# First loads of a fused attention and FFN kernel: x0 in column halves, value weights right behind it, and a new order of the first TensorE steps

## The chip, the cores and the metric

The kernel runs on one core of one Trainium2 chip. The metric is the device time of one execution in microseconds (us); lower is better. Five engines work from queues of their own: TensorE (PE in the profile), VectorE (DVE), ScalarE (ACT), GpSimd (POOL) and SyncE (SP). SP and ACT also issue the DMA transfers.

## What is computed

Two branches over the same tokens x (2048 x 640, bf16), mixed by a gate for each token:

```python
def _A_ref(x, wqkv, w_phi, wo):                      # linear attention, 32 heads of 20
    qkv = transpose(reshape(x @ wqkv, (B, S, 3, H, Dh)), (2, 0, 3, 1, 4))
    q, k, v = qkv
    pq = einsum("bhsd,hdf->bhsf", q, w_phi);  pk = einsum("bhsd,hdf->bhsf", k, w_phi)
    phi_q = concat([softmax(pq), softmax(-pq)]);  phi_k = concat([softmax(pk), softmax(-pk)])
    kv = einsum("bhsf,bhsd->bhfd", phi_k, v);  z = einsum("bhsf->bhf", phi_k)
    o = einsum("bhqf,bhfd->bhqd", phi_q, kv) / (einsum("bhqf,bhf->bhq", phi_q, z) + 1e-6)
    return o_as_rows @ wo

g = sigmoid((x * gate_w).sum(-1))
a = _A_ref(x, wqkv, w_phi, wo)
b = (silu(x @ w_gate) * (x @ w_up)) @ w_down         # F = 1728
out = g * a + (1 - g) * b
```

## The kernel before

The 2048 tokens are 16 tiles of 128, and the 640 features are five slices of 128. The value weights `wvg` hold five rows of tiles `w0` to `w4` (128 x 640 each, 160 KB), one for each slice of features, and one more column for the gate weight. A value tile V of a token tile is then ten matmuls: for each slice c, one of 320 columns (half 0) and one of 321 columns (half 1, which ends with the gate column), both with slice c of the transposed tokens `xT` as weights.

Two strings at the top of the file fix the order. `LOADS` (L33) is the order in which the loads are issued; each item goes to the queue that `XQ`, `WQ` (L391, L392) or its own function names. `ORDER` (L38) is the order in which the compute steps are recorded; every engine runs its instructions in that order. A tracker puts semaphore waits in front of an instruction for what it reads and writes. It tracks PSUM by whole banks and SBUF by byte ranges, so that the gate column of `wvg` is apart from the rest.

The steps at the start of `ORDER`:

- `H` (`warm`, L511): two matmuls of 128 x 128 on a constant, whose result nobody reads. There are 13 of these steps, so 26 matmuls.
- `X` (`xpose`, L495): transposes a token tile on TensorE. The first four tiles are loaded by rows (`load_x`, L399) and transposed this way; the other twelve are loaded by DMA transposes (`load_xt`). For tiles 0 to 2 the transposes are two parts, slice 0 and slices 1 to 4, in two PSUM banks, and each part has a copy into `xT`. `X0.0` is the first part of tile 0 and `X0.1` the second; the copies run on DVE, that of `X0.1` on ACT.
- `G` (`gcol`, L505): one matmul that turns the gate row `gwr` (loaded as 5 x 128, item `g`) into a column, and a DVE copy of it into `wvg`'s last column.
- `U` (`vpart`, L539): `Ut.c` is slice c of the value tile of token tile t, two matmuls. The tiles 0 to 2 are made in these parts, interleaved as the weights arrive.
- `h` (`load_phi`, L417): issues two small loads from ACT, behind a wait for the row tile `w3`.

PSUM is handed out as four pairs of banks by a ring (`next_pair`, L489), each step taking the pair used longest ago; an accumulating `U` tile holds its pair until its last part.

The loads of the first microseconds, by queue, in order of issue: SP has x0, g, w1, w2, w3, then the first 384 columns of the FFN weights (`f0`: wg, wu), then the DMA transposes (`k0`, `k1`, `t4` and so on). ACT has w0, x1, x2, x3, w4. A DMA issue occupies its queue for some 0.4 us.

After the start, TensorE runs through the key weights (`M`: blocks of w_phi times the transposed wqkv), the FFN's first half (`F`), keys, queries and the output steps. These are not touched.

Of the kernel before, what the change touches and what calls it, by code (L numbers as in the profile page):

```python
# [6 lines left out]
P = 128  # L7
S_TOK = 2048
D = 640
# [21 lines left out]


LOADS = """  # L33
x0 w0 x1 g w1 x2 w2 x3 w3 w4 f0 k0 k1 t4 k2 k3 k4 k5 t5 t6 t7 t8 t9 t10 t11 t12 t13 t14 t15 q0 q1 q2 q3 q4 q5
 f1 f2
"""

ORDER = """  # L38
H0 H1 H2 H3 H4 H5 H6 H7 H8 H9 H10 H11 H12 X0.0 G X0.1 X1 h U0.0 U1.0 U0.1 X2 U1.1 U2.0 U0.2 U1.2
U2.1 X3 U2.2 U0.3 U1.3 U2.3 U0.4 U1.4 U2.4 V3 Y i4 F0.1 M0 M1 F0.2 M2 V4 M3 M4 F0.0 M5 K0 i3 K1 S0 I  # L40
P0 K3 S1 P1 F1.0 K2 V6 E0 V8 K4 S2 S3 E1 S4 K5 S5 P2 P3 V7 E2 V5 R0 K6 P4 P5 R2 E3 K7 S6 E4 V15 K8
E5 V10 S7 P6 K9 E6 R1 P7 S8 K10 S9 E7 K11 S10 V9 V11 P8 E8 K12 P9 R3 E9 P10 K13 S11 E10 K14 S12 P11
# [11 lines left out]
class _Tracker:  # L54
# [90 lines left out]
    def run(self, eng, fn, reads=(), writes=(), dma=False):  # L145
        rkeys = list(dict.fromkeys(k for a in reads for k in self.keys_of(a)))
        wkeys = list(dict.fromkeys(k for a in writes for k in self.keys_of(a)))
        need = {}

        def req(ev, raw):  # L150
            if ev is None:
                return
            s, v = ev
            if s == eng and not dma and (eng == "pe" or not raw):
                return
            if v > need.get(s, 0):
                need[s] = v

        for k in rkeys:
            for kk in self._conflicts(k):  # L160
                req(self.lastw[kk], True)
                if k[0] == "psum":
                    for s, v in self.readers[kk].items():
                        req((s, v), False)
        for k in wkeys:
            for kk in self._conflicts(k):
                req(self.lastw[kk], True)
                for s, v in self.readers[kk].items():
                    req((s, v), False)
        self._wait(eng, need)  # L170
        ins = fn()
        if dma:
            sn = "d%d" % self.ndma
            self.ndma += 1
            self._add_sem(sn)
            inc = 16
        else:
            sn, inc = eng, 1
        ins.then_inc(self.sem[sn], inc)
        self.cnt[sn] += inc  # L180
        v = self.cnt[sn]
        snap = dict(self.known[eng])
        if not dma:
            snap[sn] = max(snap.get(sn, 0), v)
        self.evknow.setdefault(sn, {})[v] = snap
        ev = (sn, v)
        for k in wkeys:
            self.lastw[k] = ev
            self.readers[k] = {}
        for k in rkeys:  # L190
            r = self.readers[k]
            if r.get(sn, 0) < v:
                r[sn] = v
        return ev


def _build(nc, A_x, A_wqkv, A_w_phi, A_wo, B_x, B_w_gate, B_w_up, B_w_down, gate_w, out):
    tr = _Tracker(nc)
    pe, act, dve, pool, sp = nc.tensor, nc.scalar, nc.vector, nc.gpsimd, nc.sync
# [83 lines left out]
    def at(name, shape, dtype, rel):  # L283
        n = mybir.dt.size(dtype)
        for s in shape[1:]:
            n *= s
        assert rel + n <= SLAB, (name, rel + n, SLAB)
        t = nc.alloc_sbuf_tensor_at(name, list(shape), dtype, offset=sbase + rel)
        tr.reg(t, "sbuf", sbase + rel)
        return t  # L290
# [4 lines left out]
    xs = at("xs", [P, NPE, D], BF16, 10752)  # L295
# [10 lines left out]
    def bank(b, c0, c1, r0=0, r1=P):  # L306
        return ps[r0:r1, b * 512 + c0:b * 512 + c1]
# [9 lines left out]
    def mm(pairs):  # L317
        reads, writes = [], []
        for p in pairs:
            reads += [p[1], p[2]]  # L320
            writes.append(p[0])

        def fn():
            last = None
            for o, l, r, st, sp_, sk in pairs:
                last = pe.matmul(o, lhsT=l, rhs=r, start=st, stop=sp_, skip_group_check=sk)  # L326
            return last
        return run("pe", fn, list({id(a): a for a in reads}.values()), writes)
# [45 lines left out]
    def dma(e, dst, src, transpose=False):  # L374
        eo = tr.eng[e]

        def fn():
            if transpose:
                return eo.dma_start_transpose(dst, src)
            return eo.dma_start(dst, src)  # L380
        rd = [src] if src.tensor.name in tr.base else []
        wr = [dst] if dst.tensor.name in tr.base else []
        return run(e, fn, rd, wr, dma=True)
# [4 lines left out]
            channel_multiplier=cm), [ap], [ap])  # L388


    XQ = ["sp", "act", "act", "act"]  # L391
    WQ = ["act", "sp", "sp", "sp", "act"]  # L392
    x2 = A_x[0]
    out2 = out[0]

    def load_rows(e, dst, c, c0):
        return dma(e, dst, A_wqkv[c * P:(c + 1) * P, c0:c0 + D])

    def load_x(t):  # L399
        dma(XQ[t], xs[:, t, :], x2[t * P:(t + 1) * P, :])  # L400

    def load_xt(t):
        dma("sp", xT[:, t, :, :], x2[t * P:(t + 1) * P, :], transpose=True)
# [7 lines left out]
    def load_wv(c):  # L411
        wv_evs.append(load_rows(WQ[c], wvg[:, c, 0:D], c, 2 * D))

# [70 lines left out]
    def used(r):  # L484
        ring["lru"].remove(r)
        ring["lru"].append(r)
        return r

    def next_pair():  # L489
        return used([r for r in ring["lru"] if r < ring["n"] and r not in held][0])  # L490
# [31 lines left out]
    def v_pairs(t, pr):  # L522
        return [(bank(2 * pr + hb, 0, 320 + hb), xT[:, t, c, :], wvg[:, c, 320 * hb:640 + hb - 320 * (1 - hb)],
                 c == 0, c == 4, False) for c in range(5) for hb in range(2)]

    def v_out(t, pr):
        i = halves(pr).rearrange("p b (h d) -> p b h d", d=DH)
        o = vbuf(t)[:, 0:H * (DH + 1)].rearrange("p (b h d) -> p b h d", b=2, d=DH + 1)[:, :, :, 0:DH]
        copy("act", o, i)
        copy("act", svec[:, t:t + 1], bank(2 * pr + 1, 320, 321))  # L530
# [6 lines left out]
    vpr = {}  # L537

    def vpart(t, c):  # L539

        if c == 0:
            vpr[t] = next_pair()
            held.add(vpr[t])
        mm(v_pairs(t, vpr[t])[2 * c:2 * c + 2])
        if c == 4:
            held.remove(used(vpr[t]))
            v_out(t, vpr[t])
# [398 lines left out]
    def kv_end():  # L946
# [4 lines left out]

    ops = {
        "H": lambda i: warm(), "i": fills, "X": xpose, "G": gcol, "U": vpart, "V": vtile,
        "M": lambda m: premult(1, m), "R": lambda m: premult(0, m),
        "K": ktile, "S": knorm, "P": kmul, "p": lambda t: kmul(t, "dve"), "E": kvtile, "x": load_x, "t": load_xt, "w": load_wv, "g": load_gate, "h": load_phi, "k": lambda m: load_wt(1, m), "q": lambda m: load_wt(0, m),
        "f": lambda i: load_ffn(FCUT[i], FCUT[i + 1]), "L": load_late_weights, "T": tail_weights, "J": gates,
        "Y": w_blocks, "I": kv_begin, "N": kv_end, "Z": z_row,
# [9 lines left out]
def bass_gated_mix__linear_kernel_hedgehog__swiglu_ffn__prompt_kernel(  # L967
    nc: bass.Bass,
    A_x: bass.AP,
    A_wqkv: bass.AP,  # L970
    A_w_phi: bass.AP,
    A_wo: bass.AP,
    B_x: bass.AP,
    B_w_gate: bass.AP,
    B_w_up: bass.AP,
    B_w_down: bass.AP,
    gate_w: bass.AP,
    out: bass.AP,
):
    _build(nc, A_x, A_wqkv, A_w_phi, A_wo, B_x, B_w_gate, B_w_up, B_w_down, gate_w, out)  # L980
# [28 lines left out]
```

## Time and profile before

| | us |
|---|---|
| median of 3 runs | 285.96 (285.23 to 286.51) |
| the profiled execution, its own time | 286.04 |
| its span, first to last instruction | 284.8 |
| first TensorE instruction starts (warm matmuls) | 0.84 |
| first transpose of x0 starts | 3.85 |
| last matmul of the program ends, about | 282.9 |
| DVE busy | 193.2 |
| POOL busy | 155.3 |
| ACT busy | 139.6 |

The span is the time from the first to the last instruction on the chip. The measured time of the same execution is 1.2 us longer. An engine's busy time is the union of its instructions; the profile models the end of a pipelined matmul, so the pace of TensorE is better read from start to start. The granted clock in the profile's rows is 1.00 in every slice.

The loads at the start, from issue to landing: x0 is issued on SP at 0.81 and takes 3.0 us, w0 on ACT at 0.80 and takes 3.2, w4 as the last of the row loads on ACT at 2.70 and takes 5.3. The first FFN weights are issued at 3.00 and 3.48 and take 6.2 and 7.2 us.

### The profile page before, as it was taken

The numbers are of one execution on the slowest core, as the hardware profiler recorded it, in microseconds if no ns is written. First come the engines' busy times: TensorE is split into PE (matmuls) and PEld (weight loads), VectorE is DVE, ScalarE is ACT, GpSimd is POOL, SyncE is SP. The second block draws the span as 40 slices with busy tenths as digits, with TensorE's granted clock in tenths as the row PEclk, the third lists the DMA queues.
The fourth block names the chain that finished last, engine by engine and source line by source line (L and its number), as shares of the span: only waits on it lengthen the run. The fifth ranks groups of instructions, "written<-read, shape, count | busy, mean of one in ns | idle before, by whom it ended". The sixth has DMA issues, their size and how long they took to land.

```text
span 284.8 us, 4696 instructions
## 1 busy us (share of the span) xinstructions
PE 281.9 (99%) x1809; PEld 156.8 (55%) x1809; DVE 193.2 (68%) x280; ACT 139.6 (49%) x241; POOL 155.3 (55%) x119
## 2 busy tenths in 40 slices
PE   8999999999999999999999999999999999999997
PEld 6666777766645445445545444554544444444766
DVE  1346667784789998979999899997878355053100
ACT  2477687786755666657746764130101675001022
POOL 6276988888167859597858744463062553100100
PEclk9999999999999999999999999999999999999999
DMA  7986679200065362022330200623547520133411
GB/s 231 232 104 129 109 136 370 86 3 0 3 218 185 78 107 51 9 52 53 60 52 3 52 4 10 138 51 71 115 139 138 76 61 7 41 78 73 122 46 46
DMA packets 62085, 25.19 MB, mean 88 GB/s; under 512 B 51023, under 2 KB 61543, under 8 KB 62063
## 3 DMA queue, kind: packets, MB, share of 16 engines
q1 hardware_dynamic: 60534, 24.03, 37.7%
q10 hardware_dynamic: 1529, 0.87, 1.1%
q8 instruction: 14, 0.23, 0.4%
q14 instruction: 8, 0.07, 0.1%
HBM read 10.16 MB, written 2.63 MB: 45 GB/s over the span
## 4 chain that ended last, share of the span: by engine, by line
PE 98%; DMA 1%; DVE 0%; issue 0%
PE ps L326 97%; DMA xs<-in_A_x_dram 1%; PE ps L338 1%; DVE osb L934 0%
## 5 line engine op out<-in xcount | busy, mean ns | idle before, releaser
L354 POOL TENSOR_TENSOR hT<-hT,us 128x512 bf16<-128x512 bf16 (+1 forms) x37 | 42.9, 1167 | 43.5 <-DVE hT L358 33.2
L326 PE MATMUL ps<-xT,wg 128*128 128x512 bf16 x260 | 64.6, 379 | 0.0
L326 PE MATMUL ps<-xT,wu 128*128 128x512 bf16 x260 | 64.6, 379 | 0.0
L354 POOL TENSOR_TENSOR ph<-eq,qc 128x1320 bf16<-128x1320 bf16 x16 | 40.3, 2521 | 31.0 <-DVE qc L673 19.8
L326 PE MATMUL ps<-wqk,xT 128*128 128x320 bf16 x320 | 47.9, 299 | 0.0
L344 ACT ACTIVATE us<-ps 128x512 bf16<-128x512 f32 (+1 forms) x56 | 33.4, 597 | 22.0 <-PE ps L326 19.8
L326 PEld LDWEIGHTS ps<-xT,wu 128*128 128x128 bf16 x260 | 25.4, 98 | 30.7
L326 PEld LDWEIGHTS ps<-xT,wg 128*128 128x128 bf16 x260 | 25.0, 98 | 28.4 <-ACT oT L344 0.6
L354 POOL TENSOR_TENSOR ekr<-ekr,krec 128x1280 bf16<-128x1280 bf16 x16 | 37.3, 2358 | 5.8 <-DVE krec L368 5.8
L344 ACT ACTIVATE eq<-ps 128x640 bf16<-128x640 f32 x32 | 22.3, 703 | 32.3 <-PE ps L326 31.2
L358 DVE SCALAR_TENSOR_TENSOR hT<-hT,ps 128x512 bf16<-128x512 bf16 (+1 forms) x37 | 25.0, 681 | 19.1 <-ACT hT L344 17.5
L326 PEld LDWEIGHTS ps<-wqk,xT 128*128 128x128 bf16 x320 | 30.4, 98 | 13.3
L354 POOL TENSOR_TENSOR hx<-hx,us 128x512 bf16<-128x512 bf16 (+1 forms) x19 | 24.1, 1272 | 22.1 <-DVE hx L358 16.3
L344 ACT ACTIVATE hT<-ps 128x512 bf16<-128x512 f32 (+1 forms) x37 | 22.0, 596 | 25.0 <-PE ps L326 24.8
L326 PE MATMUL ps<-hT,wd 128*128 128x512 bf16 (+1 forms) x140 | 31.1, 379 | 0.0
L365 DVE TENSOR_REDUCE ksum<-ekr 128x64 f32<-128x1280 bf16 x16 | 23.4, 1464 | 11.0 <-ACT ekr L344 11.0
L344 ACT ACTIVATE ekr<-ps 128x640 bf16<-128x640 f32 x32 | 22.3, 703 | 6.9 <-PE ps L326 6.4
L326 PE MATMUL ps<-wvg,xT 128*128 128x320 bf16 (+1 forms) x160 | 24.7, 305 | 0.0
L365 DVE TENSOR_REDUCE qw<-ez 128x64 f32<-128x1280 bf16 x16 | 23.6, 1476 | 0.0
L365 DVE TENSOR_REDUCE qz<-eq 128x64 f32<-128x1280 bf16 x16 | 23.6, 1478 | 0.0
L354 DVE TENSOR_TENSOR ez<-eq,zb 128x1280 bf16<-128x1280 bf16 x16 | 22.9, 1449 | 0.6 <-DMA zb<-zrow 0.6
L326 PEld LDWEIGHTS ps<-hT,wd 128*128 128x128 bf16 (+1 forms) x140 | 13.0, 97 | 16.1 <-issue 1.3
(103 smaller groups left out, 291.2 us busy)
## 6 DMA issues: line engine op xcount, KB each, us to landing
wd<-in_B_w_down_dram SPq DMA_DIRECT2D x1, 2080.0 KB, 10.3
out_dram<-osb SPq DMA_DIRECT2D x2, 640.0 KB, 3.5
wg<-in_B_w_gate_dram SPq DMA_DIRECT2D x1, 1040.0 KB, 8.6
wu<-in_B_w_up_dram SPq DMA_DIRECT2D x1, 1040.0 KB, 9.8
wog<-in_A_wo_dram SPq DMA_DIRECT2D x2, 375.0 KB, 4.1
wg<-in_B_w_gate_dram SPq DMA_DIRECT2D x1, 640.0 KB, 5.0
wu<-in_B_w_up_dram SPq DMA_DIRECT2D x1, 640.0 KB, 6.3
omgb<-omgd SPq DMA_DIRECT2D x2, 256.0 KB, 4.0
```

The costliest lines, as they stand in the source:

```text
L326: last = pe.matmul(o, lhsT=l, rhs=r, start=st, stop=sp_, skip_group_check=sk)
L338: last = pe.transpose(o, i, ident[0:k, 0:k])
L344: return run("act", lambda: act.activation(o, i, func, scale=scale), rd, [o])
L354: return run(e, lambda: eo.tensor_tensor(o, a, b, op), [a, b], [o])
L358: return run("dve", lambda: dve.scalar_tensor_tensor(out=o, in0=a, scalar=s, in1=b, op0=op0, op1=op1), rd, [o])
L365: return run("dve", lambda: dve.tensor_reduce(o, i, AX.X, ALU.add), [i], [o])
```

## The change

```diff
 LOADS = """
-x0 w0 x1 g w1 x2 w2 x3 w3 w4 f0 k0 k1 t4 ...
+x0 w0 w1 x1 g x2 w2 x3 w3 w4 f0 k0 k1 t4 ...

 ORDER = """
-H0 H1 H2 H3 H4 H5 H6 H7 H8 H9 H10 H11 H12 X0.0 G X0.1 X1 h U0.0 U1.0 U0.1 X2 U1.1 U2.0 U0.2 U1.2
+H0 H1 H2 H3 H4 H5 H6 H7 H8 H9 H10 H11 X0.0 X0.1 G U0.0 U0.1 X1 h U1.0 X2 U1.1 U2.0 U0.2 U1.2

-    XQ = ["sp", "act", "act", "act"]
-    WQ = ["act", "sp", "sp", "sp", "act"]
+    XQ = ["sp", "act", "act", "sp"]
+    WQ = ["act", "sp", "sp", "sp", "sp"]

     def load_x(t):
-        dma(XQ[t], xs[:, t, :], x2[t * P:(t + 1) * P, :])
+        if t == 0:
+            for e, c0, c1 in (("sp", 0, 384), ("act", 384, D)):
+                dma(e, xs[:, t, c0:c1], x2[t * P:(t + 1) * P, c0:c1])
+        else:
+            dma(XQ[t], xs[:, t, :], x2[t * P:(t + 1) * P, :])

     def vpart(t, c):
...
-        mm(v_pairs(t, vpr[t])[2 * c:2 * c + 2])
+        vp = v_pairs(t, vpr[t])[2 * c:2 * c + 2]
+        for m in ([vp[0:1], vp[1:2]] if t == c == 0 else [vp]):
+            mm(m)
```

Tile x0 is loaded in two parts: columns 0 to 383 (98 KB) at the head of SP's queue, columns 384 to 639 (66 KB) at the head of ACT's. By queue the order is now: SP has x0's first part, w1, g, w2, x3, w3, w4, wg, wu and then the DMA transposes; ACT has x0's second part, w0, x1, x2. So x3 and w4 have moved from ACT to SP.

On TensorE there are 24 warm matmuls instead of 26. The two parts of tile 0's transposes follow each other, G comes behind them, then both matmuls of U0.0 and of U0.1, then X1, then U1.0. From X2 on the order is the old one. U0.0's two matmuls are two groups with waits of their own: the first reads half 0 of `w0`, the second half 1 and the gate column. With one H step less, the ring hands other pairs of banks to the steps behind; the number of pairs and their order of reuse are the same.

More of the change, by code (lines that the diff above doesn't have):

```diff
@@ L33 @@
 LOADS = """
-x0 w0 x1 g w1 x2 w2 x3 w3 w4 f0 k0 k1 t4 k2 k3 k4 k5 t5 t6 t7 t8 t9 t10 t11 t12 t13 t14 t15 q0 q1 q2 q3 q4 q5
+x0 w0 w1 x1 g x2 w2 x3 w3 w4 f0 k0 k1 t4 k2 k3 k4 k5 t5 t6 t7 t8 t9 t10 t11 t12 t13 t14 t15 q0 q1 q2 q3 q4 q5
  f1 f2
```

## The prediction, made before the changed kernel was run

> **What bounds the kernel now.** I read the page first, for the engine shares, then the chain of waits, then the timeline of the first 13 us, because the diff touches nothing later. The page, and under it the chain in order of time (start, length, what):
>
> ```profile
> PE 281.9 (99%) x1809; PEld 156.8 (55%) x1809; DVE 193.2 (68%) x280; ACT 139.6 (49%) x241; POOL 155.3 (55%) x119
> ```
>
> ```profile
> 0.81 3.00 DMA xs<-in_A_x_dram
> ...
> 75.52 207.36 PE ps L326 x1114
> ```
>
> TensorE is busy 281.9 of 284.8 us. The rest is 0.84 us before its first instruction and 1.9 us after its last, so inside there is about 0.1 us of idle time. No other engine can shorten the run; the diff can act only on when TensorE gets its first real operand, on waits it then meets, and on its pace. The timeline, TensorE rows (start, length, group, idle before it):
>
> ```profile
> 0.84 2.93 PE L518 MATMUL ps<-const-bfloat16-1.0 128*128 128x128 bf16 x26 [0.84 <-PEq L994]
> 3.85 0.29 PE L338 MATMUL ps<-ident,xs 128*128 128x128 bf16 x1
> 4.12 0.19 PE L326 MATMUL ps<-ident,gwr 128*128 128x5 bf16 x1
> 4.17 1.12 PE L338 MATMUL ps<-ident,xs 128*128 128x128 bf16 x9
> 5.08 1.67 PE L326 MATMUL ps<-wvg,xT 128*128 128x320 bf16 x6
> 6.59 0.44 PE L338 MATMUL ps<-ident,xs 128*128 128x128 bf16 x5
> 6.87 1.53 PE L326 MATMUL ps<-wvg,xT 128*128 128x320 bf16 x10
> ```
>
> The 26 warm matmuls end at 3.77 and x0's first transpose starts at 3.85, when its load landed (0.81 + 3.00). Of the 26, one takes 2.93/26 = 0.113. The next rows show two paces. Nine transposes start over 4.17 to 5.08, about 0.107 each, and the six value matmuls go at 0.27 each. From 6.59 on five transposes need 0.28 (0.055 each) and ten value matmuls 1.36 (0.137 each). So TensorE doubles its pace between 6.16 and 6.59, I take 6.4, though the granted clock stands at 1.00 in every row. Work ahead of that moment costs double; work after it costs half.
>
> The loads, from issue to landing, those issued at 0.80 (two) and those at 1.24 to 1.66 (three):
>
> ```profile
> wvg<-in_A_wqkv_dram ACTq DMA_DIRECT2D x1, 160.0 KB, 3.2
> xs<-in_A_x_dram SPq DMA_DIRECT2D x1, 160.0 KB, 3.0
> ```
>
> ```profile
> xs<-in_A_x_dram ACTq DMA_DIRECT2D x1, 160.0 KB, 3.1
> wvg<-in_A_wqkv_dram SPq DMA_DIRECT2D x1, 160.0 KB, 3.1
> ```
>
> With the same view on the later issues, landings are: SP queue x0 3.81, w1 4.76, w2 6.4, w3 7.2, wg 9.2; ACT queue w0 4.0, x1 4.34, x2 5.8, x3 7.0, w4 8.0. What the DMA engines moved (last column GB/s):
>
> ```profile
> 0.80:2.50 1.70, 1.66 (x16) 1.69 (x17) 0.00 (x0) 0.00 (x0) 1.27 (x9) 1.00 0.28 35
> 2.50:2.75 0.25, 0.25 (x5) 0.25 (x4) 0.00 (x0) 0.00 (x0) 0.25 (x1) 1.00 0.87 297
> 2.75:3.00 0.25, 0.25 (x5) 0.25 (x4) 0.00 (x0) 0.00 (x0) 0.25 (x1) 1.00 1.07 394
> 3.00:3.25 0.25, 0.25 (x6) 0.25 (x3) 0.00 (x0) 0.06 (x1) 0.25 (x2) 1.00 1.09 387
> ```
>
> Summed: 60 KB by 2.50, 134 by 2.75, 232 by 3.00, 329 by 3.25. One tile is 164 thousand bytes, x0 and w0 together 328: their last bytes move at about 3.25, and x0 counts as landed 0.56 later.
>
> **The change, part by part.**
>
> *x0 in column halves (98 and 66 KB) at the heads of both queues.* All of x0 is now the first 164 KB, moved by about 2.83; plus 0.56 it lands at 3.4. If instead the slow stretch to 2.5 is a cost per row (each queue still begins with 128 rows), it lands at 3.81 as before. I take 3.4, because the windows show full rate from 2.75 on.
>
> *One H item less: 24 warm matmuls.* They end at 0.84 + 24 x 0.113 = 3.55, 0.23 earlier. With x0 there, the first transpose starts at 3.60 instead of 3.85: gain 0.25. With x0 at 3.81: 0, and the gap is 0.3 of idle instead.
>
> *X0.1 ahead of G.* Five transposes at 0.107: TensorE reaches G at 4.14 (4.39 in the late case). G needs gwr. Its issue moves from second to third on SP, behind w1. I place each new landing on its queue by bytes ahead of it, interpolated between the old landings. w1 is now bytes 98 to 262 on SP; old x0 ended at 164 (3.81) and old w1 at 328 (4.76), so w1 lands at 3.81 + 0.6 x 0.95 = 4.4. The gate row came at most 0.27 after the tile ahead of it (x0 3.81, G's weights wanted it until 4.12 less the 0.04 to start): 4.4 to 4.65, I take 4.55. Ends: 4.08 as before (no wait at all), and 5.0 if w1 keeps its 4.76. So a **new wait at G of 0.4** (0 to 0.85), and behind it on TensorE stands everything. DVE's copy of the gate column and ACT's copies have nothing else to do then.
>
> *U0.0 split into its two matmuls.* The first does not touch the gate column and goes right behind G at 4.60, 0.27 long; w0, by the same interpolation on ACT (230 KB; 4.0 and 4.34), is there at 4.1. The second needs DVE's copy of G: before, G began at 4.12 and the cast was done at 4.53, 0.41 later, so now at 4.96, and the matmul at 5.02: a wait of 0.15 (0 to 0.2). The extra signal between the two: nothing I can see, at most 0.05.
>
> *U0.0 and U0.1 ahead of X1, U1.0 behind it.* Same instructions. U0.0's second and U0.1's two: 5.02 + 3 x 0.27 = 5.83. X1's transposes (x1 lands at 4.9): to 6.37. U1.0 needs X1's first slice copied: transpose and drain 0.33, DVE 0.22, about 6.44, when TensorE is at its fast pace: to 6.71. Before, the same set (ten transposes, G, six matmuls) was done when X2 started, 6.59. That is **+0.12**. Then X2 (x2 lands at 6.3 on ACT; 0.28) to 6.99, and U1.1 needs the copy of X1's other four slices: 6.37 + 0.2 + 0.43 = 7.0 plus 0.06, before done at 5.76 and a full us early. **+0.08**. U2.0 and later waits have cover: X2's copies end at 7.7 and U2.1 comes at 8.2.
>
> *The other moved issues.* x3 and w4 go to SP, two issues of 0.43 ahead of wg, wu and the first DMA transposes. Hidden: wg landed at 9.2 for matmuls at 11.78, wu at 10.7 for 12.86, wT's second block at 12.97 for about 14.3, its last at 19.3 for 20.95. The thinnest cover is 1.3 against a shift of 0.86; without it the path would get up to 0.86. On SP x3 lands at 6.9 for X3 at 8.3, w2 at 5.7, w3 at 7.6 for U0.3 near 9, w4 at 8.3 for 9.6. The w_phi load waits for w3, so it may come 0.4 later, against 0.9 between its first block product and M0. ACT issues one load less before its table load, which ends near 4.0 instead of 4.47, ahead of the copy that X0.1 feeds.
>
> **Sum.** +0.12 + 0.08 = +0.2 us. Ends: with gwr at 4.08 and the early start, about -0.25; with gwr at 5.0, +0.65. The profiled execution took 286.04 (span 284.8 and 1.2 around it), 0.08 above the median 285.96 of the runs shown. So 286.24 by its own time, and against the median **286.15**. The three runs lie 1.28 apart, which is more than the whole sum; about 0.5% (1.4 us) is what can be told from no change here.
>
> **Rivals.**
> (a) *The pace doubles later.* The slow pace lasted from 0.84 to 6.4, over a stretch in which TensorE was idle for only 0.1 us. Now it idles 0.05 + 0.4 + 0.15 = 0.6 us between 3.55 and 5.02. If the step needs unbroken work, the count starts anew with them: from their end, 5.02 + 5.5 = 10.5, the step comes 4.1 us later and half of that is lost, +2.0; from their beginning, 3.55 + 5.5 = 9.05, 2.65 later, +1.3. The middle of the two is +1.7: **287.65**. It decides from the point where the idle share is too large; the before run shows only that 0.1 us is allowed. For it: no row shows a wait of 0.4 being tolerated. Against it: each wait is short beside the stretch. The Trainium skill, "TensorE: Matmul & The Clock Gate", Part 1, says that one busy window of about 3.4 us releases the clock and that the window runs free of the kernel's start; by that an estimate for a spoiled window is half of 3.4, +1.7, and the before trace agrees so far that work at the start ran at half pace for 5.5 us. How busy is busy enough, no run here shows.
> (b) *The gain comes through.* gwr, being tiny, lands as early as before; G does not wait, the start gain of 0.25 stays: **285.7**. For it: gwr came close behind x0. Against it: it now has w1 in front on SP.
> (c) *The change does not do what it says:* x0 still lands at 3.81, the start is at 3.85, G waits only 0.15, all later waits stay: G goes at 4.55 either way, so again +0.2, 286.15, with the step at 3.60 wrong. It shares the forecast's time.
>
> **Chances.** Forecast with (c) 0.62, (b) 0.18, (a) 0.17, other 0.03. Forecast and (b) lie within 0.5%, (a) beyond it. The runs of before lie 0.73 below to 0.55 above their median, so from (b) I move 0.07 to faster by over 0.5% (below 284.5), and from the forecast 0.02 to slower (above 287.4): 0.07, 0.74 between, 0.19. Range 285.2 to 287.3: (b) less half a us of run spread, over the forecast's upper bound 286.6, to 0.35 short of (a).
>
> **What would show it.** First transpose at 3.60 (not 3.85); the gate matmul near 4.6 with an idle gap ahead of it released by gwr's DMA; U0.0's second matmul waiting for DVE; X2's transposes near 6.7; the pace step near 6.4. If value matmuls still go at 0.27 at 7 us, (a) has it. If G starts before 4.25, (b). If a wait appears at the first wT matmuls after 13.9, my cover for SP's later issues was wrong.

## The result, and the profile after

| | before | changed |
|---|---|---|
| median of 22 runs each, us | 285.96 (285.21 to 286.51) | 286.48 (285.58 to 288.60) |
| ratio changed to before | 1 | 1.0031, 95% interval 1.0016 to 1.0045 |
| the profiled execution, its own time (span) | 286.04 (284.8) | 286.56 (285.3) |

The ratio is that of the averages. In this comparison the changed kernel is slower by 0.3%, which is clear of zero and below the 0.5% named as no change. The median moved by +0.5; the spread grew from 1.3 to 3.0 us.

The page of the changed kernel:

```profile
PE 280.7 (98%) x1800; PEld 156.2 (55%) x1807; DVE 190.8 (67%) x280; ACT 139.6 (49%) x241; POOL 156.0 (55%) x119
```

Over the span the page gives TensorE 1.7 us more idle time than before (285.3 less 280.7, against 284.8 less 281.9), though a few matmul records are missing in it (1800, with 1807 weight loads). Between 0.84 and 6.5 us it is 1.35 us more. Where it idles, the chain of waits shows (start, length, what):

```profile
1.72 3.70 DMA gwr<-in_gate_w_dram
...
5.46 0.19 PE ps L326
...
5.68 0.19 DVE wvg L350
...
5.92 0.58 PE ps L326 x3
...
6.59 0.23 DVE xT L350
```

Before, the chain hung on x0's load and then on TensorE alone. Now it hangs on the gate row, issued at 1.72 and landed at 5.42, and twice on a DVE copy: that of the gate column and that of X1's first slice. The timeline of TensorE:

```profile
0.84 2.72 PE L522 MATMUL ps<-const-bfloat16-1.0 128*128 128x128 bf16 x24 [0.84 <-PEq L1000]
3.36 0.74 PE L338 MATMUL ps<-ident,xs 128*128 128x128 bf16 x5
5.46 0.18 PE L326 MATMUL ps<-ident,gwr 128*128 128x5 bf16 x1 [1.37 <-DMA gwr<-in_gate_w_dram]
5.56 0.94 PE L326 MATMUL ps<-wvg,xT 128*128 128x320 bf16 x4
6.34 0.44 PE L338 MATMUL ps<-ident,xs 128*128 128x128 bf16 x5
6.87 0.45 PE L326 MATMUL ps<-wvg,xT 128*128 128x320 bf16 x2
7.16 0.44 PE L338 MATMUL ps<-ident,xs 128*128 128x128 bf16 x5
```

The first transpose starts at 3.36 instead of 3.85, and then the gate matmul waits 1.37. X2's transposes start at 7.16 instead of 6.59; the last matmul's copy starts at 283.46 instead of 282.91. That +0.55 is the whole difference of the two profiled executions (0.52 by their times), and it arises before 7.2 us. The three value matmuls from 5.92 to 6.34 take 0.14 each, and X1's five transposes have the length of X2's (0.44 with the end of the last, against 0.74 at 3.36): here the pace doubled while TensorE was waiting, at or before 5.56 (each of the eleven recorded value matmuls up to 8 us takes 0.30 to 0.31, where those ahead of the doubling in the other traces take 0.42 and more), against about 6.5 in the profile before. That took back part of the loss.

The loads, from issue (0.80, then 1.25) to landing, and the DMA rate of both kernels (last column GB/s), first the changed kernel's:

```profile
xs<-in_A_x_dram SPq DMA_DIRECT2D x1, 96.0 KB, 2.1
xs<-in_A_x_dram ACTq DMA_DIRECT2D x1, 64.0 KB, 2.3
```

```profile
wvg<-in_A_wqkv_dram ACTq DMA_DIRECT2D x1, 160.0 KB, 4.0
wvg<-in_A_wqkv_dram SPq DMA_DIRECT2D x1, 160.0 KB, 3.8
```

```profile
0.80:2.50 1.70, 1.66 (x16) 1.69 (x17) 0.00 (x0) 0.00 (x0) 1.27 (x9) 1.00 0.38 101
2.50:3.25 0.75, 0.75 (x9) 0.75 (x8) 0.00 (x0) 0.55 (x1) 0.75 (x2) 1.00 0.79 196
3.25:4.25 1.00, 0.84 (x8) 0.58 (x6) 0.22 (x1) 0.85 (x2) 0.94 (x3) 1.00 1.01 334
```

The same stretches of the kernel before:

```profile
2.50:3.25 0.75, 0.75 (x10) 0.75 (x8) 0.00 (x0) 0.06 (x1) 0.75 (x2) 1.00 1.01 360
3.25:4.25 1.00, 0.92 (x9) 0.49 (x8) 0.07 (x1) 1.00 (x1) 0.94 (x3) 1.00 1.09 376
```

x0 is there at 3.1, 0.7 earlier than before. But from 2.5 to 3.25 the engines move 196 GB/s instead of 360, though they are 0.79 busy. By 2.5 the changed kernel is ahead (101 x 1.7 = 172 KB against 60); by 4.25 it is behind (653 KB against 706). w0 lands at 5.25 and w1 at 5.05, against 4.0 and 4.76 before.

### The profile page after: what moved, and what is told of

It reads as the page before. It is cut to its first block, busy times and chain, and to the rows that moved or that the text cites. A ratio compares the mean times of both kernels' runs of the same rounds, so it can differ in the third digit from the quotient of the medians.

```text
span 285.3 us, 4687 instructions
## 1 busy us (share of the span) xinstructions
PE 280.7 (98%) x1800; PEld 156.2 (55%) x1807; DVE 190.8 (67%) x280; ACT 139.6 (49%) x241; POOL 156.0 (55%) x119
## 3 DMA queue, kind: packets, MB, share of 16 engines
HBM read 10.16 MB, written 2.63 MB: 45 GB/s over the span
## 4 chain that ended last, share of the span: by engine, by line
PE 97%; DMA 1%; issue 0%; DVE 0%; POOL 0%; POOLq 0%
PE ps L326 97%; DMA gwr<-in_gate_w_dram 1%; PE ps L338 0%; DVE osb L940 0%; POOL ident L386 0%; DVE xT L350 0%; POOL gwr L372 0%; DVE wvg L350 0%; POOL ident L372 0%; POOLq L386 0%; POOL bmask L372 0%; POOLq L1000 0%
## 5 line engine op out<-in xcount | busy, mean ns | idle before, releaser
L354 POOL TENSOR_TENSOR hT<-hT,us 128x512 bf16<-128x512 bf16 (+1 forms) x37 | 43.6, 1184 | 45.0 <-DVE hT L358 33.6
L354 DVE TENSOR_TENSOR ez<-eq,zb 128x1280 bf16<-128x1280 bf16 x16 | 22.1, 1395 | 0.2 <-DMA zb<-zrow 0.2
(103 smaller groups left out, 287.9 us busy)
```

The source lines that it names most:

```text
L354: return run(e, lambda: eo.tensor_tensor(o, a, b, op), [a, b], [o])
```

## The experiments

Each of them ran beside the kernel before on the same chip. "Upper group" below means executions of 287.3 us or more; most kernels have a gap near there, and so a ratio of the averages can differ from that of the medians. Of 115 executions of the kernel before, 3 lie in it. The runs were spread over two chips: on one the second run of the changed kernel, the gate row early, the order alone with 24 warm matmuls and the fill of the changed kernel, on the other the rest; the kernel before has 2 of 35 and 1 of 58 in the upper group there.

### The changed kernel again, and a third trace

The kernel is the same.

> The changed kernel once more, for a second trace and more times. Theory T1 (where each load lands is a matter of queue order): the gate row lands near 5.4 us again and the gate matmul waits 1.2 to 1.5 us, the median is 286.3 to 286.7. Rival R1 (the landing at 5.4 was one bad draw of the DMA engines): it lands anywhere from 4.4 to 5.4. Either way I expect single times from 285.6 to 288.6.

Median 286.13 over 12 executions (285.71 to 288.04), ratio 1.0011 (0.9992 to 1.0031), which is not clear of zero. The gate row landed at 4.5 this time; TensorE's rows of this second trace:

```profile
4.52 0.19 PE L326 MATMUL ps<-ident,gwr 128*128 128x5 bf16 x1 [0.42 <-DMA gwr<-in_gate_w_dram]
4.62 0.94 PE L326 MATMUL ps<-wvg,xT 128*128 128x320 bf16 x4
5.93 0.45 PE L338 MATMUL ps<-ident,xs 128*128 128x128 bf16 x5 [0.36 <-DMA xs<-in_A_x_dram]
```

Here the gate matmul waits 0.42, and X1 then waits 0.36 for x1, which landed at 5.9. R1 holds, and T1 falls: where a load lands is not settled by the queue order alone.

> One more look at the changed kernel: whether the gate row lands early (4.5, as in the second trace) or late (5.4, as in the first), and when the pace doubles. By T2 a time of 286.8 or less shows value matmuls at 0.14 us by 6.5 us, and a time of 287.3 or more shows them at 0.27 until 8 us or later.

286.07 us; gate matmul at 4.56, x1 at 4.9, value matmuls fast before 6.5. Over the three traces X2 starts at 7.16, 6.76 and 6.65 (before: 6.59), in executions of 286.56, 286.19 and 286.07. In all three the pace had doubled by 5.6. None of them fell in the upper group, in which 8 of the 35 executions of the changed kernel lie; of that group of this kernel there is no trace.

### Does idle time on TensorE delay the doubling of its pace?

The cleanest test takes the kernel before and only takes warm matmuls away. Nothing that is needed moves.

```diff
-H0 H1 H2 H3 H4 H5 H6 H7 H8 H9 H10 H11 H12 X0.0 G
+H0 H1 H2 H3 H4 H5 H6 H7 H8 X0.0 G
```

> The kernel before with 18 warm matmuls instead of 26: they end at 2.9 instead of 3.8, and x0 still lands at 3.8, so that no needed work moves and TensorE only idles for 0.9 us ahead of it. Theory T2: the pace doubles later in a good part of the executions; at least 4 of 12 above 286.9, the median 0.2 to 1.5 above that of before. Rival R2 (an idle stretch of this length costs nothing by itself): the median within 0.2 of before and the spread as before, 285.3 to 286.7.

Median 287.06 against 285.81; seven of 12 executions above 286.9, ratio 1.0041 (1.0022 to 1.0060). TensorE's rows:

```profile
3.72 0.29 PE L338 MATMUL ps<-ident,xs 128*128 128x128 bf16 x1 [0.80 <-DMA xs<-in_A_x_dram]
...
5.13 1.81 PE L326 MATMUL ps<-wvg,xT 128*128 128x320 bf16 x6
6.73 0.74 PE L338 MATMUL ps<-ident,xs 128*128 128x128 bf16 x5
7.27 2.80 PE L326 MATMUL ps<-wvg,xT 128*128 128x320 bf16 x10
9.90 0.44 PE L338 MATMUL ps<-ident,xs 128*128 128x128 bf16 x5
```

x0's first transpose starts even earlier than before, at 3.72, after 0.80 of idle time. The six value matmuls end at 6.73, against 6.59 before. But the ten from 7.27 take 2.63 until the next row instead of 1.36: the slow pace lasts until about 9.7. The view gives the granted clock as 1.00 here too, as it does for the slow stretch of the kernel before, so that number does not tell the two paces apart. This execution took 287.67, 1.6 us more than the profiled one before, and no needed work was late by more than 0.14: idle time alone costs that. T2 is shown for this place. One thing in the trace was not touched and still moved: w1 landed at 6.17 instead of 4.76, with the same loads in the same order, just in time for U0.1.

Next, the gate row moved ahead of w1 in the changed kernel:

```diff
-x0 w0 w1 x1 g x2 w2
+x0 w0 g w1 x1 x2 w2
```

> The gate row issued second on SP, ahead of w1 (as before the change); all else as in the changed kernel. Theory T3 (the gate row is late only because it stands behind w1): it lands near 3.5 to 4.1, the gate matmul does not wait, and the wait moves to the first value matmul, which wants w0: near 5.2 if w0 is as late as in the changed kernel. Gain then 0.1 to 0.4 us against the changed kernel, 286.1 to 286.4. Rival R3 (w0 and w1 were late because of the gate row's few packets between them): w0 lands near 4.2 and the time falls to 285.7 or below.

Median 287.71; ratio 1.0045 (1.0027 to 1.0064). Its executions fall in two groups, five at 286.3 to 286.7 and seven at 287.6 to 288.3. The trace is of the second:

```profile
3.89 0.21 PE L326 MATMUL ps<-ident,gwr 128*128 128x5 bf16 x1
3.99 0.86 PE L326 MATMUL ps<-wvg,xT 128*128 128x320 bf16 x2
6.12 0.69 PE L326 MATMUL ps<-wvg,xT 128*128 128x320 bf16 x2 [1.26 <-DMA wvg<-in_A_wqkv_dram]
...
8.28 2.18 PE L326 MATMUL ps<-wvg,xT 128*128 128x320 bf16 x10
```

The gate matmul no longer waits, and w0 was there as well, at 3.55; the wait moved to w1, which landed at 5.98. The pace doubles near 9.6. Neither T3 (wait for w0, gain) nor R3 (gain) came about: it got slower. Filling that wait in this kernel:

```diff
-U0.0 U0.1 X1
+U0.0 H13 U0.1 X1     # H13: 12 warm matmuls in one step
```

> The kernel with the gate row early, and twelve warm matmuls between U0.0 and U0.1, where TensorE waits for w1 for about 1.3 us. Without them 7 of 12 executions took 287.6 to 288.3 and 5 took 286.3 to 286.7. Theory T2 (a wait in this stretch makes the doubling of TensorE's pace miss in part of the executions and come one period later): the upper group goes away, at most 2 of 12 above 287.3, the median is 286.4 to 286.9. Rival R2 (the upper group is later loads): still about half of the executions above 287.3, and the trace shows U0.1 later than 6.2 in them.

One of 11 executions above 287.3 instead of seven of 12; median 286.79, ratio 1.0034 (1.0016 to 1.0051). The trace has no gap, and the ten value matmuls take 1.36. As T2 expects, the upper group all but went, and the lower one stayed: the wait itself still costs. The two runs of this pair were on different chips. The same in the changed kernel, between X0.1 and G:

```diff
-X0.0 X0.1 G U0.0
+X0.0 X0.1 H13 G U0.0
```

> Twelve warm matmuls put between X0.1 and G, in the time in which TensorE waits for the gate row; the loads and all else as in the changed kernel. Theory T2 (the idle time at 4 to 5.4 us makes the doubling of TensorE's pace come late in part of the executions, and this is the upper tail): the times above 287 go away, the spread falls to about that of before (1.3 us), the median falls to 285.9 to 286.2. Rival R2 (the tail and the median come from loads landing later in some executions, and the wait is simply lost time): the spread stays near 3 us and the median stays at 286.4 or above, since the gate matmul still starts near 5.4.

The spread fell from 3.0 to 1.5 us and one of 12 executions is in the upper group, but the median is 286.50, not 286.2 or less. In its trace w1 landed at 4.45, and the twelve fillers kept TensorE until 5.17. In the other traces of this order the gate row came 0.25 to 0.4 behind w1; by that it was there near 4.8 (an estimate), and the fillers pushed the gate matmul back. T2 got the spread right; on the median it missed. With 8 of 35 against 1 of 12 the fall of the upper group is not clear of chance here; in the pair before it (7 of 12 against 1 of 11) chance alone would do it about 3 times in 100.

### Which part of the change costs?

The order of the steps alone, with the old loads:

```diff
+ ORDER of the changed kernel (24 warm matmuls, X0.1 ahead of G, U0.1 ahead of X1)
  LOADS, XQ, WQ and load_x as before
```

> The loads of before on their old queues in their old order, with the changed order of TensorE's steps, the split of U0.0 and 24 warm matmuls. Theory T4 (the loads' new order is what costs): x0 lands at 3.8, the gate row at 4.1, w1 at 4.8; no wait over 0.3 us, 285.8 to 286.2, spread as before. Rival R4 (the new order of the TensorE steps costs, through the waits for DVE's copies): 286.4 or above.

Median 285.86 against 286.0, ratio 0.9993 (0.9977 to 1.0009): as T4 has it, no cost of the order that can be told from nothing. Its profiled execution, at 287.61, is the one of 13 in the upper group (x0 waited for 0.34, the pace doubles near 9.4). With two more warm matmuls (`H12` back in):

> The kernel with the order alone changed (the loads as before), with 26 warm matmuls instead of 24, so that TensorE hardly idles before x0 at 3.8. By T2 no execution above 287.0 or at most one, and by the gate wait of 0.16 that the order removes, less the new waits for DVE: 285.6 to 286.0, the same as before or up to 0.3 faster. If it is above 286.2, the order costs after all.

Median 286.15 against 285.87, ratio 1.0024 (1.0003 to 1.0045), with two of 12 in the upper group (288.04 and 288.91). T2 expected one at most, and 285.6 to 286.0; both are misses. TensorE idles for only 0.06 us in its trace, which is not of the upper group; what those two did is not known. Without them the median is 286.1, 0.2 above that of before: between this run and the one before it, a cost of the order of 0 to 0.2 us stays open.

x0 in halves alone, in the kernel before:

```diff
-        dma(XQ[t], xs[:, t, :], x2[t * P:(t + 1) * P, :])
+        if t == 0:      # columns 0:384 on SP, 384:640 on ACT
+            ...
```

> The kernel before with x0 alone changed: two column parts at the heads of both queues; w0 comes second on ACT, gate row and w1 second and third on SP, 26 warm matmuls and the old order of steps. Theory T5 (whatever stands right behind x0 pays for x0's earlier landing, because the first reads of the weight rows run slow): x0 lands near 3.0, the DMA rate dips below 250 GB/s between 2.5 and 3.5, w0 and x1 land later than 4.0 and 4.3 and the time is that of before or up to 0.5 above. Rival R5 (the lateness of w0 and w1 is due to both standing second at once): w0 lands near 4.0 and x1 near 4.3, no dip, and the time is 285.7 to 286.0.

Median 288.3, ratio 1.0074 (1.0050 to 1.0099), nine of 12 in the upper group: the worst of all that were repeated. The trace is of the fastest of the twelve (286.24), so it does not show what held up the others. In it x0 landed at 3.3 and w0 already at 3.55, but x1 at 5.65, and X1 waited 1.36 for it. T5's dip and its late x1 came, but w0 was not late, and the median is far above what T5 or R5 allowed: both fall. The rate (GB/s last):

```profile
2.50:3.00 0.50, 0.50 (x7) 0.50 (x6) 0.00 (x0) 0.00 (x0) 0.50 (x1) 1.00 1.16 355
3.00:3.25 0.25, 0.25 (x5) 0.25 (x3) 0.00 (x0) 0.00 (x0) 0.25 (x2) 1.00 0.89 179
3.25:4.00 0.75, 0.75 (x10) 0.75 (x9) 0.08 (x1) 0.32 (x1) 0.69 (x3) 1.00 0.76 142
```

The slow stretch is here too, later and deeper. The other half of the loads' change: x0 whole again, and all else as changed.

```diff
-        if t == 0:
+        if t < 0:       # never: x0 whole, on SP
```

> The changed kernel with x0 whole at the head of SP again; ACT begins with w0. The queues are then SP: x0, w1, gate row, w2, x3, w3, w4; ACT: w0, x1, x2; order and 24 warm matmuls as in the changed kernel. Theory T6 (the halves at both heads are what makes the following tiles late): x0 at 3.8, w0 at 4.0, x1 at 4.4, w1 and the gate row at 4.5 to 4.8, no dip between 2.5 and 3.75, waits of 0.3 before x0 and 0.2 to 0.4 at the gate matmul, 285.8 to 286.2 with up to 3 of 12 above 287 through the wait before x0. Rival R7 (w1 ahead of the gate row is what costs): the gate matmul waits until 5 or later and the median is 286.4 or above.

x0 at 3.8, w0 at 3.9, x1 at 4.75; the gate matmul at 4.84 after a wait of 0.32; rates of 352 and 369 GB/s where the changed kernel has 196 and 334. So far T6, and R7's wait until 5 or later did not come. The lower group (five executions, 285.94 to 286.48, median 286.07) is where T6 put the kernel; but seven of 12 are in the upper one, where T6 had three at most, so the median is 287.45, ratio 1.0042 (1.0024 to 1.0061). The trace is of the lower group; its two short waits, 0.25 ahead of x0 and 0.32 at the gate matmul, may be what splits the executions, but whether those of the upper group waited longer is not shown.

### What is the slow stretch?

Token tiles instead of weight rows behind x0's halves:

```diff
-x0 w0 w1 x1 g x2 w2 x3
+x0 x1 x2 g w0 w1 w2 x3     # x1 on SP, x2 and w0, w2 on ACT
```

> The changed kernel with x1 and x2 second on the queues (SP: x0's part, x1, gate row, w1; ACT: x0's part, x2, w0, w2); the steps keep the changed order, so TensorE waits longer for the gate row and w0 and the time is no matter here: 286.5 to 288.5. Theory T5 (the weight rows are what runs slow): no dip between 2.5 and 3.25, rates of 300 and more until about 500 KB are moved, the dip comes when w0 and w1 start. Rival R6 (the dip comes because both halves of x0 end at once and both queues move on together, whatever follows): a dip below 230 GB/s between 2.5 and 3.25 with token tiles too.

289.11 us in one execution, with TensorE waiting 2.1 for w0. The rate:

```profile
2.50:3.25 0.75, 0.75 (x10) 0.75 (x8) 0.00 (x0) 0.55 (x1) 0.75 (x2) 1.00 1.05 319
3.25:3.75 0.50, 0.50 (x7) 0.50 (x6) 0.04 (x1) 0.50 (x1) 0.44 (x3) 1.00 1.02 307
3.75:4.25 0.50, 0.35 (x4) 0.08 (x1) 0.18 (x1) 0.34 (x2) 0.50 (x1) 1.00 0.75 195
```

No dip between 2.5 and 3.25, and one when w0 and w1 come up: R6 falls, T5 fits this trace. But with the halves alone and with the gate row early, w0 landed at 3.55 (in the halves-only kernel at 355 GB/s, the row above) and the dip came behind it, when w1 and x1 came up. What causes it stays open.

This trace also shows the clock change. The four value matmuls from 6.68 to 7.23 go at the fast pace (0.14 each), the ten from 8.67 to 11.35 at the slow one (0.27). Here the view shows it in the granted clock (third figure from the end):

```profile
6.60:7.90 1.30, 1.12 (x10) 0.79 (x11) 0.42 (x2) 0.00 (x0) 0.00 (x0) 1.00 0.93 298
7.90:11.30 3.40, 3.40 (x17) 2.15 (x16) 0.88 (x3) 0.00 (x0) 0.00 (x0) 0.51 1.22 249
```

So the doubled pace is not kept for good: some 1.2 us after the wait of 2.14 us it fell back to half for 3.4 us, in which TensorE was busy throughout. By these rows that costs about 1.7 us (half of 3.4, an estimate) beside the wait itself.

A last order, with x1 and w0 right behind the halves:

```diff
-x0 w0 w1 x1 g x2 w2 x3          X0.0 X0.1 G U0.0 U0.1 X1 h U1.0 X2
+x0 g x1 w0 w1 x2 w2 x3          X0.0 X0.1 G X1 h U0.0 U1.0 U0.1 X2
 # w0 on SP, x1 and w1 on ACT
```

> x0 in halves, then the gate row and w0 on SP and x1 on ACT right behind, w1 and x2 next; order X0.0 X0.1 G X1 U0.0 U1.0 U0.1, 24 warm matmuls. By T5 x1 lands near 4, w0 near 4.8; TensorE waits 0.2 to 0.5 for x1 and as much for w0, in pieces: 285.8 to 286.4, a few executions above 287. If the weight rows do not run slow here (R5), both land by 4.3 and it is 285.5 to 285.8, faster than before by up to 0.4.

x1 at 3.55 as hoped, but w0 at 5.55, after a stretch of 147 GB/s from 3.25 to 4.0; eight of 12 in the upper group, median 287.52, ratio 1.0047 (1.0024 to 1.0070). None of the orders tried beats the kernel before.

## Why the prediction was right, and where its steps were off

The forecast, no change within 0.5% with 286.15 and a range of 285.2 to 287.3, held: 286.48, and 286.13 in the second comparison. Part of that is luck, as the fourth point says. All of it plays before 7.5 us, as forecast, and the gate row is what the path waits for.

- **The start** was better than forecast: 3.36 instead of 3.60. x0 landed at 3.1, not 3.4, and the last warm matmul frees TensorE one start-to-start step (24 of them from 0.84 to 3.36, 0.105 each) after it begins, not at the end of its row; the 0.113 of the prediction has that last end in it. Gain 0.49 instead of 0.25.
- **The step that failed is the gate row's landing** (and w0's and w1's): 4.55 forecast by bytes ahead on the queue, 5.42 in the first trace, 4.5 in the other two. The wait at G was 0.4 in the sum and measured 1.37, 0.42 and 0.47. My interpolation took the rate of the kernel before; it held in the two traces for gate row and w1 (4.15 and 4.25; forecast 4.4) but not for x1, forecast at 4.9 and landed at 5.63, 5.9 and 4.9. The rate was not that of before: each of the four traces with this order of loads has the stretch of low rate behind x0's halves.
- **The waits for DVE** came where they were forecast: U0.0's second matmul behind the gate column (0.29 of weight-load idle time in the first trace, 0.15 forecast) and U1.0 behind X1's copy (0.27, where the sum had 0.07, since X1's transposes took half as long).
- **The pace** was to double near 6.4, and the sum had U0.0's second matmul, U0.1 and X1 at the slow pace: 1.42 us from 5.02 to U1.0 at 6.44. In the first trace they ran at the fast one, 0.95 us from 5.92 to 6.87. That took back 0.47 of the 0.91 by which the gate matmul was later than forecast (5.46, not 4.55). No step of the prediction gave this, so it is luck: with the forecast's pace this execution would have been about 1.0 above before instead of 0.55, near 287.1 (an estimate from these rows). In the traces of the lower groups the doubling came by 5.3 (x0 whole) to about 6.5 (before), so a few tenths between two single traces may be the moment of the doubling and not the change.
- **The sum** +0.2 against +0.55, +0.15 and about 0 in the three profiled executions (286.56, 286.19, 286.07 against 286.04). Over all 35 executions of the changed kernel the lower group has its median at 286.2, +0.3 on the 285.9 of before. The path was right; its largest term was mis-sized in the first trace, and the early doubling, which no term had, made up for half of that.
- **SP's later issues**, x3 and w4 ahead of the FFN weights: wg landed at 9.3 (before 9.2), and no wait for wT appears at 14.51, where its first matmul goes. The cover held.
- **Rival (a)**, the pace that doubles later, had 0.17 as if it were all or nothing. It is real, but it takes some executions and leaves others: 8 of 35. Its price of 1.7 is the distance of the two groups (mean 287.9 against 286.2). On top of the forecast's 286.15 it makes 287.85; the 287.65 of the prediction left its own 0.2 out. 8/35 x 1.7 = 0.4 on the mean, a little more than the lower group's shift. That the wait splits the executions was not forecast; the range held only the part of them below 287.3.
- **Rival (c)** is out: the halves did bring x0 earlier. **Rival (b)** needed the gate row at 4.1, and in none of the three traces of the changed kernel did it come before 4.5.

The table puts TensorE's idle time between 0.84 and 6.5 us, as read from the busy time in that window of each trace, beside the share of the upper group:

| kernel | idle in the trace, us | 287.3 or more |
|---|---|---|
| gate early, filled; changed, filled | 0.0 | 1 of 11; 1 of 12 |
| order only, 26 warm; before | 0.1 | 2 of 12; 3 of 115 |
| order only, 24 warm | 0.35 | 1 of 13 |
| changed (three traces) | 0.6, 0.9, 1.4 | 8 of 35 |
| x0 whole | 0.7 | 7 of 12 |
| less warm | 1.0 | 4 of 12 |
| x1 first; gate early; halves only | 1.1; 1.3; 1.4 | 8, 7 and 9 of 12 |

Up to 0.35 us it is 8 of 163, from 0.6 on 43 of 95. The idle time of one traced execution is not that of the others, and the kernels ran on two chips, so this is a tendency, not a threshold. That idle time causes it is shown by the kernel with less warm matmuls, whose trace is of the upper group; the filled pair (7 of 12 against 1 of 11) agrees. For the other kernels, the changed one among them, it is argued from the tendency: none of the changed kernel's upper executions has a trace.

## What to carry to other kernels

In a kernel that one engine bounds from its first microsecond, getting the first operand earlier is worth only as much as the second and third operands follow it; split one load and look at where all the others land, in several traces, since a landing can move by 0.9 us from one execution to the next (w1 of the changed kernel: 4.15 to 5.05), and by 1.4 in the kernels whose loads were left alone (4.76 to 6.17). An early wait on TensorE has a second price beside its length, because the doubling of its pace may come 3 us later in part of the executions; cover it with work that nobody needs. The fill of the early-gate kernel took 0.9 off its median; that of the changed kernel took nothing off, and in its trace it was longer than the wait. Compare distributions, not only medians, when a change makes waits in the warm-up.

## What the runs showed of the hardware that was not expected

The doubling of the pace does not always wait for unbroken work: in all three traces of the changed kernel it came while TensorE was waiting, or within a few tenths of a us after. In other executions the same sort of wait put it off from about 6.5 us to 9.2 to 9.7 (x1 first, order only, gate early, less warm), 2.7 to 3.2 us later. And it can be taken back: with x1 and x2 second, the pace was doubled before 6.7 and half again from 7.9 to 11.3, for 3.4 us at a granted clock of 0.51. The mean granted clock of that execution is 0.994. Ten of the 51 upper executions of the table have the same mean, all of them at 288.1 us or more. So the upper group may be of two kinds, a late doubling and a fall back; none of these ten has a trace. The two groups of times lie 1.5 to 1.7 us apart (gate early: means 286.5 and 287.9; changed: 286.2 and 287.9), half of 2.9 to 3.5 us. The Trainium skill, "TensorE: Matmul & The Clock Gate", Part 1, describes a window of about 3.4 us that runs free of the kernel's start, and that a busy one releases the clock; the distance and the stretch of 3.4 us agree, and a free-running window would explain why one kernel falls in both groups. How much idle time spoils a window is not stated there, and these runs give only the tendency above.

A load split over both queues brought its tile 0.5 to 0.8 us earlier in every trace, but a stretch of 0.5 to 0.75 us at 140 to 220 GB/s followed it in each, at a place where the unsplit kernels ran at 335 and more. They in turn are slow at the very start: 30 to 70 KB by 2.5 us, against 120 to 180. Why the engines are slow there while 0.6 to 0.9 busy was not found.
